# Top-k attention with a leaky-ReLU MLP: the first MLP chunks started earlier, half a layer summed ahead, two units scored later

## Chip, cores and metric

One core of a Trainium2 chip runs the whole program. The metric is device time in microseconds (us), as the median of repeated runs. Five engines take part, each with a queue that it works off in order: PE (TensorE, matrix products), DVE (VectorE), ACT (ScalarE), POOL (GpSimd) and SP, which only issues transfers here.

## What is computed

Attention over 8 batches, 8 heads, 576 tokens and head size 64, where each query keeps only the keys with its 32 highest scores; then a two-layer MLP over the 4608 tokens that this gives.

```python
scores = (1.0 / np.sqrt(D)) * np.matmul(q, k.transpose(0, 1, 3, 2))
kth = np.partition(scores, -32, axis=-1)[..., -32:-31]
scores = np.where(scores >= kth, scores, -1000000000.0)
scores = scores - np.max(scores, axis=-1, keepdims=True)
attn = np.exp(scores)
attn = attn / (np.sum(attn, axis=-1, keepdims=True) + 1e-09)
x = np.matmul(attn, v)              # (B, H, S, D) -> (B*S, H*D) = (4608, 512)
h = x @ w_in                        # w_in (512, 2048)
out = np.maximum(0.01 * h, h) @ w_out   # w_out (2048, 512)
```

All products are made in float32, which PE does in two passes; a matmul of the program is two rows of the profile.

## The kernel before

**Units and steps.** Heads go in pairs, four pairs a batch (`HP`). A unit is 128 query rows of both heads of one pair: 16 whole units a batch, and 2 made of the 64 rows left over from two pairs each, 144 units in all. Even batches have their whole units first, ordered by block of 128 queries and then by pair, so units 0 to 3 are the first 128 tokens of batch 0, 4 to 7 the next 128, 8 to 11 and 12 to 15 the last two blocks; 16 and 17 are its left-over units, 18 and 19 those of batch 1. The program is written out by a Python loop over steps `s` (L538), in an order fixed by hand. Every engine's queue gets its instructions in the order in which that loop emits them.

**What a step emits.** In step s DVE finds the top 32 of unit s (`top_k`, L243): it folds both halves of the scores to maxima and minima (L250), then four rounds of MAX8 (L255) and three of MATCH_REPLACE8 (L258); `slot()` emits one round, so a step has four slots. POOL masks unit s-1 (L268, L269, one pass for each head); ACT makes its exponents and their sums (`exponents`, L272; `sums`, tile `ze`, L277). Unit s-2 is divided by its sums: DVE's reciprocal (L281, tile `rz`) and ACT's normalising (L284), together `weights_of`. Then its weights are transposed, in one of two ways. `transpose` (L286) has ACT split them in two 16-bit halves (L293), SP store both to memory (L294) and a transfer bring them back transposed (L298, tile `wT`). `transpose_in_haste` (L300) has PE transpose nine blocks (L308), and ACT copy them out (`keep_transposed`, L314); units in `HASTY` go this way. Later, at the place that `values_at` (L449) gives, PE multiplies the transposed weights by the values (L335) for two units, and ACT copies the result to the MLP's input `x` (L349). A place is (step, MIDDLE) or (step, END). At the end of even steps PE makes the scores of the next two units (`scores`, L203: two tiles `wide`, and one `narrow` that both units share, L220), and ACT copies them out (L227). `first_scores` (L229) makes one unit's scores in two `wide` tiles without `narrow` (L236, L241); before, it serves units 0 and 1 only.

**Where the reciprocal stands.** `weights_of` comes at one of three spots of a step: ahead of the first slot for units in `HURRIED` below step 20 (`at_first`); after the first slot from step 20 on and in steps next to a hurried unit; after the second slot otherwise (`late`). DVE's queue is in order, so a reciprocal that has to wait for its sum holds up the top-k behind it.

**The MLP.** Tokens go in chunks: two of 128, then seventeen of 256 (`CHUNKS`). Chunk 0 needs units 0 to 3, chunk 1 units 4 to 7, chunk 2 (tokens 256 to 511) units 8 to 15. `mlp` is a generator that emits a few matmuls at a time: first layer (L359 and transposes L375 for the two small chunks, L391 for the others, tile `ph`), leaky ReLU by ACT (Prelu, L364 and L397, to `gT`), second layer (L403, tile `pz`), copy and store (L412, L413). A step has seven places at which `mlp_steps(budget)` lets it emit matmuls until the budget, counted in columns, is used up. Until chunk 2 is ready the budget is `EARLY_SHARE` a place; after that what is left is spread evenly over the steps until the next chunk is ready. A chunk becomes ready when its last values are copied (`attended`).

**On-chip accumulators.** The pool `ps_sc` has two buffers `wide` and one `narrow`, of two banks each; `ps_ml` has two of one bank for the MLP (tag `ml`). A tile that takes a buffer waits until the buffer's last reader is done.

The lines that set the places before:

```python
    LAG = 3
    HURRY = 20
    HURRIED = (15, 23, 31)
    HASTY = (14, 15, 23, 31)
    UNHURRIED = 14
    def values_at(n):
        if n < UNHURRIED:
            return (n | 1) + LAG + 1, MIDDLE
        return (n | 1) + LAG - ((n | 1) in HURRIED), END
```

Of the kernel before, what the change touches and what calls it, by code (L numbers as in the profile page):

```python
# [20 lines left out]
def kernel(  # L21
# [13 lines left out]
    nc = tc.nc  # L35
# [158 lines left out]
    units = []  # L194
    for b in range(B):
        first = b % 2 == 1
        whole = [Unit(b, [b * HP + hp], q0 + LEFT * first)
                 for q0 in range(0, S - LEFT, P) for hp in range(HP)]
        left = [Unit(b, [b * HP + hp, b * HP + hp + 1], 0 if first else S - LEFT)
                for hp in range(0, HP, 2)]  # L200
        units += left + whole if first else whole + left
# [27 lines left out]
    def first_scores(u):  # L229

        ps = [ps_sc.tile([P, 2, 512], F32, name="wide", bufs=2) for i in range(2)]
        for half in range(2):
            for i, pi, side, r0 in u.parts:
                qt, kt = qk_of[pi]
                d = slice(side * D, (side + 1) * D)
                nc.tensor.matmul(ps[i][:, half, 0:HS], qt[d, u.q0:u.q0 + P],  # L236
                                 kt[d, half * HS:(half + 1) * HS], start=True, stop=True)
        u.both = work.tile([P, 2, S], F32, name="s_sb", bufs=5)
        u.s = [u.both[:, i, :] for i in range(2)]
        for i in range(2):  # L240
            nc.scalar.copy(u.s[i].rearrange("p (h n) -> p h n", h=2), ps[i][:, :, 0:HS])  # L241
# [130 lines left out]
    def turned(j, g_of):  # L372
# [3 lines left out]
        nc.scalar.copy(gT[:, 4 * j:4 * (j + 1), 0:P], pt)  # L376
        yield 2 * P

    def mlp(ch):

        n = CHUNKS[ch]
        t0 = sum(CHUNKS[:ch])
        x = x_of[ch]
        if ch < EARLY:
            yield from hidden_of_few(ch, x)
        for f0 in range(0, NFC if ch >= EARLY else 0, 2):
            ph = ps_ml.tile([P, 2, CHMAX], F32, name="ph", tag="ml")
            for i in range(2):
                f = f0 + i
                for c in range(HP):  # L390
                    nc.tensor.matmul(  # L391
                        ph[:, i, 0:n], w_in[c][:, f * P:(f + 1) * P], x[c][:, 0:n],
                        start=(c == 0), stop=(c == HP - 1),
                    )
                    if c == 1 or i == 0 and c == HP - 1:
# [29 lines left out]
    def mlp_steps(budget):  # L425
        owed[0] += budget
        while owed[0] > 0:
            if running[0] is None:
                if not ready:
                    owed[0] = 0.0  # L430
                    return
                running[0] = mlp(ready.pop(0))
# [8 lines left out]

    LAG = 3
    HURRY = 20
    HURRIED = (15, 23, 31)
    HASTY = (14, 15, 23, 31)
    UNHURRIED = 14
    MIDDLE, END = 0, 1

    def values_at(n):  # L449

        if n < UNHURRIED:
            return (n | 1) + LAG + 1, MIDDLE
        return (n | 1) + LAG - ((n | 1) in HURRIED), END

    steps = units

# [11 lines left out]
    def attended(*place):  # L468
        for at, ch in ready_at:
            if at == place:  # L470
                ready.append(ch)
                backlog[0] += mlp_cost(ch)

    def slot_budget(s):

# [3 lines left out]
            return EARLY_SHARE  # L479
        return backlog[0] / ((until + 1 - s) * SLOTS)  # L480

    EARLY_SHARE = 500
    SLOTS = 7

    with tc.manual_schedule():
# [51 lines left out]

        for s in range(len(steps) + LAG + 1):  # L538
            cur, old, older, new = unit(s), unit(s - 1), unit(s - 2), ()
            if s % 2 == 0:  # L540
                new = [u for u in steps[s + 2:s + 4] if u]
            picks = top_k(cur) if cur else iter(())
            budget = slot_budget(s)

            def slot():
                next(picks, None)

            at_first = s < HURRY and s - 2 in HURRIED
            if at_first:
                weights_of(older)  # L550
            slot()
            if old:
                mask(old, 0)
                mask(old, 1)
            late = s < HURRY and not {s - 1, s - 2} & set(HURRIED)
            if older and not late and not at_first:
                weights_of(older)
            mlp_steps(budget)
            weighed = values(s, MIDDLE)
            at_once = s - 2 in HURRIED or any(at == (s, MIDDLE) for at, _ in ready_at)  # L560
# [24 lines left out]
            if new and s < HURRY:  # L585
                scores(new)
            keep(values(s, END), s, END)
            if new and s >= HURRY:
                scores(new)
            budget = slot_budget(s + 1)  # L590
            mlp_steps(budget)
            load_more(s)
# [59 lines left out]
```

## Time and profile before

| what | value |
|---|---|
| median of 6 runs | 1470.53 us (1469.16 to 1472.89) |
| the profiled execution | 1470.42 us, span 1468.5 us |
| PE busy | 1393.5 us (95%) |
| DVE busy | 1321.7 us (90%) |
| ACT, POOL busy | 1097.8 and 1096.1 us (75% each) |
| second layer, L403 | 504.7 us, 1152 passes |
| first layer of the large chunks, L391 | 482.6 us, 2176 passes |
| idle DVE ahead of the reciprocals, L281 | 45.3 us |

The span is what the profiler saw of the program's instructions; the execution's time holds some 2 us more around it. In the chain of work that ended last PE has 79% and DVE 14%. A row of the timeline gives start and length in us, engine, line, operation, output and inputs, shapes, the number of instructions merged, and in brackets idle time before and what ended it. A row of waits gives the engine that waited, for whom, the total, the number of times and the longest.

### The profile page before, as it was taken

The page shows a single profiled execution, that of the slowest core. Times are in us where ns is not written, and L with a number is a line of the kernel's source. Part 1 is how long each engine was busy: PE and PEld are TensorE (multiplying, and loading weights), DVE is VectorE, ACT ScalarE, POOL GpSimd, SP SyncE. Part 2 cuts the span into 40 slices and gives each one's busy share as a digit, 9 for nine tenths or more (in the row PEclk, how much of TensorE's full clock was granted, in tenths as well). Part 3 has the DMA queues.
Part 4 walks back from the last instruction along what each step waited for, and adds up shares of the span by engine and source line. Part 5 has one row for each costly group of instructions (what it writes and reads, how often), then busy time and mean ns, then how long its engine had stood idle before and what let it go on. Part 6 is the DMA issues. An engine that isn't in the chain of part 4 may idle for free.

```text
span 1468.5 us, 24096 instructions
## 1 busy us (share of the span) xinstructions
PE 1393.5 (95%) x8068; PEld 927.9 (63%) x8068; DVE 1321.7 (90%) x3400; ACT 1097.8 (75%) x1979; POOL 1096.1 (75%) x743
## 2 busy tenths in 40 slices
PE   7717999999999999999999999999999999999999
PEld 2304548575767676767676767666666666666674
DVE  7999999999999999999999999999999999999600
ACT  8657888777887777777777777777777777777710
POOL 3288888888788888788888887878787878787700
PEclk9957999999999999999999999999999999999999
DMA  9724443655376455664566555666457545554510
GB/s 347 284 74 129 144 120 100 187 145 144 96 193 190 137 137 155 171 185 137 146 165 187 149 137 138 179 178 152 124 163 207 137 137 138 162 139 135 146 47 14
DMA packets 388796, 222.30 MB, mean 151 GB/s; under 512 B 333888, under 2 KB 333889, under 8 KB 386625
## 3 DMA queue, kind: packets, MB, share of 16 engines
q1 hardware_dynamic: 388672, 220.77, 53.4%
q8 instruction: 63, 1.03, 0.3%
q14 instruction: 61, 0.49, 0.1%
HBM read 46.14 MB, written 92.01 MB: 94 GB/s over the span
## 4 chain that ended last, share of the span: by engine, by line
PE 79%; DVE 14%; DMA 3%; ACT 2%; issue 1%; SPq 0%; POOL 0%; DVEq 0%; ACTq 0%
PE pz L403 31%; PE ph L391 30%; PE wide L335 10%; DVE tops L255 6%; PE wide L220 6%; DVE pairs L258 5%; PE narrow L220 3%; DMA raw<-in_weights_dram 2%; DVE pairs L250 2%; DMA wT<-apart 1%; DMA apart<-split 0%; ACT split L293 0%; DVE scale L152 0%; DVE w_out L155 0%; ACT wT L127 0%
## 5 line engine op out<-in xcount | busy, mean ns | idle before, releaser
L268 POOL TENSOR_SCALAR pen<-s_sb,tops 128x576 f32<-128x576 f32 x288 | 637.5, 2213 | 208.6 <-DVE tops L255 139.3
L255 DVE MAX8 tops<-pairs 128x8 f32<-128x288 f32 (+1 forms) x1152 | 635.8, 591 | 0.0
L403 PE MATMUL pz<-w_out,gT 128*128 128x512 f32 x1152 | 504.7, 594 | 2.4 <-ACT scale L364 2.4
L391 PE MATMUL ph<-x,w_in 128*128 128x256 f32 x2176 | 482.6, 381 | 0.0
L258 DVE MATCH_REPLACE8 pairs<-tops,pairs 128x288 f32<-128x288 f32 (+1 forms) x864 | 460.1, 538 | 0.0
L391 PEld LDWEIGHTS ph<-x,w_in 128*128 128x128 f32 x2176 | 409.5, 190 | 76.4 <-issue 22.2
L269 POOL TENSOR_TENSOR s_sb<-s_sb,pen 128x576 f32<-128x576 f32 x288 | 406.5, 1411 | 24.1
L403 PEld LDWEIGHTS pz<-w_out,gT 128*128 128x128 f32 x1152 | 216.4, 190 | 267.2 <-issue 262.8
L293 ACT COPY split<-s_sb 128x1152 uint16<-128x1152 uint16 x280 | 309.4, 1146 | 0.0
L284 ACT ACTIVATE s_sb<-s_sb,rz 128x576 f32<-128x576 f32 x288 | 207.6, 773 | 45.2 <-DVE rz L281 45.1
L272 ACT ACTIVATE s_sb<-s_sb,nbias 128x576 f32<-128x576 f32 x288 | 222.2, 772 | 13.8 <-POOL s_sb L269 13.8
L250 DVE TENSOR_TENSOR pairs<-s_sb 128x576 f32<-128x576 f32 x288 | 213.4, 779 | 9.9
L335 PEld LDWEIGHTS wide<-wT,vt 128*64 128x64 f32 x3200 | 161.7, 139 | 67.5 <-issue 34.8
L335 PE MATMUL wide<-wT,vt 128*64 128x128 f32 (+1 forms) x3200 | 179.4, 268 | 25.5 <-ACT s_sb L227 22.2
L227 ACT COPY s_sb<-wide 128x704 f32<-128x704 f32 x142 | 107.1, 754 | 21.4 <-PE wide L220 21.4
L397 ACT ACTIVATE gT<-ph 128x512 f32<-128x512 f32 x136 | 80.6, 592 | 54.2 <-PE ph L391 53.4
L349 ACT COPY x<-wide 128x128 f32<-128x128 f32 (+1 forms) x160 | 32.2, 260 | 112.8 <-PE wide L335 112.8
L220 PE MATMUL wide<-kt,qt 64*128 64x352 f32 (+1 forms) x392 | 75.1, 493 | 26.0 <-ACT s_sb L227 23.5
L412 ACT COPY o_sb<-pz 128x512 f32<-128x512 f32 x36 | 21.0, 584 | 97.6 <-PE pz L403 97.6
L227 ACT COPY s_sb<-narrow 128x448 f32<-128x448 f32 x142 | 68.7, 536 | 0.7
L281 DVE RECIPROCAL rz<-ze 128x2 f32<-128x2 f32 x144 | 22.2, 154 | 45.4 <-ACT ze L277 45.3
L258 DVE MATCH_VALUE_LOAD pairs<-tops,pairs 128x8 f32 x864 | 62.5, 72 | 0.0
(63 smaller groups left out, 621.7 us busy)
## 6 DMA issues: line engine op xcount, KB each, us to landing
apart<-split SPq DMA_DIRECT2D x280, 288.0 KB, 2.1
raw<-in_weights_dram SPq DMA_DIRECT2D x16, 1024.0 KB, 6.9
vt<-in_vk_dram SPq DMA_DIRECT2D x32, 320.0 KB, 3.4
out_dram<-o_sb SPq DMA_DIRECT2D x36, 256.0 KB, 2.6
qt<-in_qT_dram SPq DMA_DIRECT2D x20, 288.0 KB, 3.1
kt<-in_kT_dram SPq DMA_DIRECT2D x20, 288.0 KB, 3.7
raw<-in_qT_dram SPq DMA_DIRECT2D x12, 288.0 KB, 3.2
raw<-in_kT_dram SPq DMA_DIRECT2D x12, 288.0 KB, 3.7
```

Of the source, the lines that this page charges most:

```text
L220: nc.tensor.matmul(to[r0:r0 + u.rows, i, :], qt[d, u.q0:u.q0 + u.rows], kt[d, k0:k1], start=True, stop=True)
L250: nc.vector.tensor_tensor(pairs[:, :, n, :], u.both[:, :, 0:HS], u.both[:, :, HS:S], op)
L255: nc.vector.max(out=u.tops[:, i, r, :], in_=rest[i])
L258: nc.vector.match_replace(out=rest[i], in_to_replace=u.tops[:, i, r, :], in_values=rest[i], imm_value=LOWEST)
L268: nc.gpsimd.tensor_scalar(pen, u.s[i], u.tops[:, i, ROUNDS - 1, 7:8], MASKED, ALU.is_lt, ALU.mult)
L269: nc.gpsimd.tensor_tensor(u.s[i], u.s[i], pen, ALU.add)
L272: nc.scalar.activation(u.s[i], u.s[i], AF.Exp, bias=u.nbias[:, i:i + 1], scale=SCALE, accum_out=u.z[:, i:i + 1])
L284: nc.scalar.activation(u.s[i], u.s[i], AF.Copy, bias=0.0, scale=u.rz[:, i:i + 1])
L293: nc.scalar.copy(split, pairs[:, :, h])
L335: nc.tensor.matmul(po[side * D:(side + 1) * D, o, :], vt[:, c, side, :], u.wT[:, c + side * NKC if c + 1 < NKC else c, r:r + n], start=(c ...
L391: nc.tensor.matmul(ph[:, i, 0:n], w_in[c][:, f * P:(f + 1) * P], x[c][:, 0:n], start=(c == 0), stop=(c == HP - 1),)
L403: nc.tensor.matmul(pz[0:m, 0:DMODEL], gT[:, f, r0:r0 + m], w_out[f // 4][:, f % 4, :], start=(f == 0), stop=(f == NFC - 1),)
```

## The change

- Chunks 0 and 1: units 2, 3 and 6, 7 join `HURRIED`, and their values are placed at (5, END) and (9, END) instead of (7, MIDDLE) and (11, MIDDLE). Units 0 to 3 and 7 join `HASTY`. `EARLY_SHARE` goes from 500 to 560.
- Units 8 to 15 are reordered so that a pair's two blocks follow each other: 8 and 9 are pair 0, 10 and 11 pair 1, and so on. So x of pairs 0 and 1 is complete over chunk 2 after unit 11, of pair 2 after 13, of pair 3 after 15.
- A new generator `begin_hidden` adds up the first half of chunk 2's first layer (8 of 16 blocks of w_in's columns) over pairs 0 and 1 from (15, MIDDLE), and over pair 2 from (17, MIDDLE). Four blocks lie in a `narrow` tile, four in both `ml` tiles, which they hold until `mlp` adds pair 3 and applies the leaky ReLU.
- As `narrow` is taken, units 18 and 19 are not scored at the end of step 16 by `scores`, but at the end of step 17, behind the values of units 14 and 15, by `first_scores`, which now also takes units of 64 rows.

```diff
+        tiles = [(0,), (P,), (2 * P, 3 * P)] if b == 0 else [(q0,) for q0 in range(0, S - LEFT, P)]
         whole = [Unit(b, [b * HP + hp], q0 + LEFT * first)
-                 for q0 in range(0, S - LEFT, P) for hp in range(HP)]
+                 for q0s in tiles for hp in range(HP) for q0 in q0s]
...
-                nc.tensor.matmul(ps[i][:, half, 0:HS], qt[d, u.q0:u.q0 + P],
+                nc.tensor.matmul(ps[i][r0:r0 + u.rows, half, 0:HS], qt[d, u.q0:u.q0 + u.rows],
                                  kt[d, half * HS:(half + 1) * HS], start=True, stop=True)
...
+    begun = {}
+
+    def begin_hidden(ch, pairs):
+        n = CHUNKS[ch]
+        x = x_of[ch]
+        if ch not in begun:
+            first = ps_sc.tile([P, 2, 512], F32, name="narrow").rearrange("p h (f n) -> p h f n", n=CHMAX)
+            begun[ch] = [first[:, 0], first[:, 1]]
+            begun[ch] += [ps_ml.tile([P, 2, CHMAX], F32, name="ph", tag="ml") for k in range(2)]
+        done = 0
+        for f in range(NFC // 2):
+            for c in pairs:
+                nc.tensor.matmul(begun[ch][f // 2][:, f % 2, 0:n], w_in[c][:, f * P:(f + 1) * P], x[c][:, 0:n],
+                                 start=(c == 0 and f % 2 == 0), stop=False)
+                done += 1
+                if done % 2 == 0:
+                    yield 2 * n
...
-            ph = ps_ml.tile([P, 2, CHMAX], F32, name="ph", tag="ml")
+            first = 0
+            if ch in begun and f0 < NFC // 2:
+                ph, first = begun[ch][f0 // 2], HP - 1
+            else:
+                ph = ps_ml.tile([P, 2, CHMAX], F32, name="ph", tag="ml")
             for i in range(2):
                 f = f0 + i
-                for c in range(HP):
+                for c in range(first, HP):
...
-    HURRIED = (15, 23, 31)
-    HASTY = (14, 15, 23, 31)
+    HURRIED = (3, 7, 15, 23, 31)
+    HASTY = (0, 1, 2, 3, 7, 14, 15, 23, 31)
     UNHURRIED = 14
+    LATE_SCORES = 17
...
-        if n < UNHURRIED:
-            return (n | 1) + LAG + 1, MIDDLE
-        return (n | 1) + LAG - ((n | 1) in HURRIED), END
+        if (n | 1) in HURRIED:
+            return (n | 1) + LAG - 1, END
+        return ((n | 1) + LAG + 1, MIDDLE) if n < UNHURRIED else ((n | 1) + LAG, END)
...
+        for last, pairs in ((11, (0, 1)), (13, (2,))):
+            if values_at(last) == place:
+                ready.append(begin_hidden(EARLY, pairs))
...
-    EARLY_SHARE = 500
+    EARLY_SHARE = 560
...
-            if s % 2 == 0:
-                new = [u for u in steps[s + 2:s + 4] if u]
+            if s % 2 == 0 and s != LATE_SCORES - 1:
+                new = steps[s + 2:s + 4]
+            elif s == LATE_SCORES:
+                new = steps[s + 1:s + 3]
...
-            at_once = s - 2 in HURRIED or any(at == (s, MIDDLE) for at, _ in ready_at)
+            at_once = s - 2 in HURRIED or s == values_at(11)[0] or any(at == (s, MIDDLE) for at, _ in ready_at)
...
-            if new and s < HURRY:
+            if new and s < HURRY and s != LATE_SCORES:
                 scores(new)
             keep(values(s, END), s, END)
             if new and s >= HURRY:
                 scores(new)
+            elif s == LATE_SCORES:
+                for u in new:
+                    first_scores(u)
```

More of the change, by code (lines that the diff above doesn't have):

```diff
@@ L386, in mlp @@
         for f0 in range(0, NFC if ch >= EARLY else 0, 2):
-            ph = ps_ml.tile([P, 2, CHMAX], F32, name="ph", tag="ml")
+            first = 0
[3 more added lines that the diff above has]
+                ph = ps_ml.tile([P, 2, CHMAX], F32, name="ph", tag="ml")
             for i in range(2):
                 f = f0 + i
-                for c in range(HP):
+                for c in range(first, HP):
                     nc.tensor.matmul(
                         ph[:, i, 0:n], w_in[c][:, f * P:(f + 1) * P], x[c][:, 0:n],
-                        start=(c == 0), stop=(c == HP - 1),
+                        start=(c == 0), stop=(c == HP - 1 and (i == 1 or not first)),
                     )
-                    if c == 1 or i == 0 and c == HP - 1:
+                    if not first and (c == 1 or i == 0 and c == HP - 1):
                         yield 2 * max(n, 225)
@@ L431, in mlp_steps @@
                     return
-                running[0] = mlp(ready.pop(0))
+                running[0] = ready.pop(0)
             cost = next(running[0], None)
@@ L470, in attended @@
             if at == place:
-                ready.append(ch)
+                ready.append(mlp(ch))
                 backlog[0] += mlp_cost(ch)
+        for last, pairs in ((11, (0, 1)), (13, (2,))):
+            if values_at(last) == place:
+                ready.append(begin_hidden(EARLY, pairs))
     def slot_budget(s):
```

## The prediction

> **What bounds the kernel now.** I number steps by the unit whose top-k runs in them; (17, END) is the end of step 17. First the windows, cut where chunks become ready (columns: busy us of PE, PEld, DVE, ACT, POOL, then granted clock).
>
> ```profile
> span 1468.5 us, 24096 instructions
> 64.90:117.80 52.90, 14.98 (x100) 11.05 (x100) 52.45 (x137) 29.33 (x52) 38.11 (x27) 0.61 0.25 68
> 117.80:224.30 106.50, 92.36 (x544) 51.19 (x546) 105.66 (x277) 86.19 (x166) 89.89 (x61) 0.94 0.46 128
> 224.30:295.20 70.90, 70.89 (x492) 49.79 (x487) 70.34 (x185) 56.06 (x109) 59.82 (x41) 1.00 0.54 148
> 295.20:369.00 73.80, 73.79 (x420) 50.35 (x419) 70.72 (x184) 55.57 (x105) 59.82 (x41) 1.00 0.52 144
> 369.00:453.00 84.00, 82.39 (x483) 55.84 (x484) 80.88 (x210) 66.90 (x126) 68.94 (x46) 1.00 0.55 156
> 453.00:1410.00 957.00, 956.42 (x5706) 654.00 (x5703) 890.94 (x2323) 746.41 (x1368) 760.82 (x509) 1.00 0.57 154
> ```
>
> From 453 on PE idles 0.6 us in 957: it is the bound, to the end. Before 118 DVE alone is full. So the question is when that full stretch begins. The chain of waits across 453 says (start, us, what):
>
> ```profile
> 439.01 2.10 ACT split L293 x2
> ...
> 441.13 4.21 DMA apart<-split
> ...
> 445.40 4.63 DMA wT<-apart
> ...
> 450.07 1.31 PE wide L335 x20
> ...
> 455.44 12.09 PE ph L391 x56
> ```
>
> At 450.07 PE waits for unit 39, the last of chunk 5, due at (42, END), and that unit hangs on DVE's step 41. Then DVE's own waits, in the window 224 to 455, and its step starts (first instruction of a top-k):
>
> ```profile
> DVE rz L281 <- ACT ze L277: 5.1, 5, 2.5
> ```
>
> ```profile
> 64.84 1.42 DVE L250 TENSOR_TENSOR pairs<-s_sb 128x576 f32<-128x576 f32 x2
> ...
> 224.26 1.45 DVE L250 TENSOR_TENSOR pairs<-s_sb 128x576 f32<-128x576 f32 x2
> ...
> 433.62 1.51 DVE L250 TENSOR_TENSOR pairs<-s_sb 128x576 f32<-128x576 f32 x2
> ```
>
> Undisturbed, DVE takes (224.26 - 64.84)/18 = 8.857 us a step; in the window 64 to 224 it waits for nothing. Step 41 would then start at 64.84 + 41 x 8.857 = 427.98 and starts at 433.62: **5.64 us lost, all of it after 224**, in reciprocals that wait for ACT's sums, ACT waiting in its queue for PE. The values at 450.07 come 16.45 after step 41's start, through ACT and two DMAs. That gives the **ceiling**: however much PE is relieved early, the full stretch can begin 5.64 sooner at most, and every DVE stall that the change adds before step 41 comes off that.
>
> PE's own rows:
>
> ```profile
> 110.81 4.53 PE L335 MATMUL wide<-wT,vt 128*64 128x128 f32 x40 [13.91 <-ACT s_sb L227]
> ...
> 149.34 2.40 PE L335 MATMUL wide<-wT,vt 128*64 128x128 f32 x40
> ...
> 210.55 1.43 PE L308 MATMUL wide<-ident,s_sb 128*128 128x128 f32 x9
> ...
> 223.77 2.40 PE L335 MATMUL wide<-wT,vt 128*64 128x128 f32 x40 [1.06 <-ACT wT L314]
> 226.10 7.17 PE L391 MATMUL ph<-x,w_in 128*128 128x256 f32 x32
> ```
>
> and one each of ACT, the copies of a whole unit's scores and a sum's end:
>
> ```profile
> 64.53 1.18 ACT L241 COPY s_sb<-wide 128x576 f32<-128x576 f32 x2 [5.86 <-PE wide L236]
> ...
> 139.61 0.20 ACT L277 ACTIVATE ze<-z 128x2 f32<-128x2 f32 x1
> ```
>
> **Part 1, the head start of chunk 2.** 24 matmuls (8 blocks of w_in by 3 pairs), two passes each, at 7.17/32 = 0.222 us (with overlap): 10.7 us leave steps 18 to 25. There PE takes 75.6 us (values at 223.77 to those at 299.36) against DVE's 8 x 8.857 = 70.9. Without 10.7, with the late scores (2.1 for two units: 217.07 to 219.17) added: 67.0, so DVE sets the pace there. Steps 26 to 33 keep 75.3 (299.36 to 374.65): PE falls 4.4 behind, where before it was 4.7 behind at step 26 with no stall yet. The nine steps of chunk 4 give that back. So of the 5.64 nearly all is open; stalls that stay: 0 to 1.1 (the first one of before, at 308), I take 0.3.
>
> **Part 2, units 18 and 19 late.** Their scores' last copy ended at 220.2, 4 before step 18; now they follow the values of 14 and 15. Times after step 17's start: POOL's mask of unit 16 is there at 3.15 (138.72 against 135.57 in step 8), the exponents take 0.95, then ACT copies unit 15's transposes (1.04): 5.2. PE meanwhile runs unit 15's nine transposes to 2.5 and the eight third-pair matmuls, 16 x 0.222 = 3.55, to 6.05. Values 2.35: 8.4. ACT copies them (0.43) to 8.85; the second tile of unit 18 is the one that they leave, so its scores (1.05) end at 9.9, and both copies (1.18) at 11.1. Step 18 should start at 8.86: **late by 2.3 plus some hops, 2.6 taken**. No gain is possible; at worst the eight matmuls slip behind ACT's copy as well, 4.5. Queued behind: DVE's whole stream, POOL's masks; unit 19's scores wait for unit 18's copies, but are due a step later.
>
> **Part 3, chunks 0 and 1 sooner.** Units 0 to 3 and 7 lose two split copies (2.10 of ACT), two stores and a DMA transpose each, and gain nine PE transposes (1.27 to 1.43) and one pair of copies (1.18). SP's queue only loses entries; loads behind them go out sooner at most. At (5, END) and (9, END) ACT's copies of the values wait for PE, and behind them in ACT's queue stand the next step's normalising and exponents, which the reciprocals need. PE has the room: 14.98 busy of 52.9. Values of 2 and 3 move from step 7 to (5, END), some 13 us earlier, of 6 and 7 from step 11 to (9, END). 560 columns a place: 1024 stand for four passes of 512, 4 x 0.438 = 1.75 us, so 7 places ask 6.7 us a step instead of 6.0. With 1.17 of values and 1.07 of scores PE has 8.94 a step where DVE takes 8.86 (8.24 before): full, 0.7 over in nine steps, 1.3 more for unit 7's transposes.
> This is paid where DVE meets ACT. Step 9 now begins with unit 7's reciprocal, step 5 with unit 3's, and in steps 4 and 8 the reciprocal moves a slot forward, from 4.5 to 2.95 after the start. In step 8 the sum came at 139.81; the new place is at 135.57 + 2.95 = 138.52, up to 1.3 too soon. From there ACT has normalise 1.35, one gT copy 0.47, exponents 0.76, splits 2.10, exponents and sum 1.1: 144.3 at the earliest, just when step 9's reciprocal wants it (144.27), so 0.2 to 0.4 late. Step 5 has copies of 1.04 in place of splits and fits. In steps 10 to 14 sums came 1.2 to 4.5 after the step's start, with 4.5 allowed; a PE some 2 us behind pushes some over. Bounds 0.2 and 4, **1.5 taken**, nearer to the low end as units 10 to 15 leave ACT time to catch up.
>
> The clock: the same 40 passes took 4.53 after 13.9 idle and 2.40 in a full stretch. With transposes and scores just ahead I take 3.2 for the first values in step 5; it lies within the 1.5. [...]
>
> **Part 4, the rest.** The units' order and the score tile's rows change no count. Two accumulators in the score tile and both others are held from step 15 to 18: chunk 1 is done by then (62 places of 560 from (5, END): step 14), and no scores fall between. If it were not, see the third rival.
>
> **Sum**: 5.64 - 0.3 - 2.6 - 1.5 = 1.2 won. The profiled execution took 1470.42 around its span of 1468.5, the median is 1470.53: **1469.3 us**, no change that can be told (0.2%, 2.9 us, is about what a measurement of this kernel can tell from none). Own range, with all lower and all upper bounds: 5.64 less 2.5 to 9.6, so 1467.3 to 1474.4.
>
> **Rivals.**
> Faster: the reciprocals cost nothing and steps 26 to 41 have no stall. Then 5.64 - 2.3 is won: 1467.1. For it: ACT is busy 86 of 106 us in 118 to 224. Against: step 9's tight chain. To be clearly faster, part 3 may cost 0.3 at most.
> Slower: the full PE of steps 6 to 14. Each Prelu in ACT's queue waits for PE, each sum behind it comes late, DVE waits, one step after another. It decides from 2.8 of stalls in steps 5 to 17 on (with 2.6 and 0.3, all of 5.64), and at 1 us a step in steps 8 to 14 it costs 7: 1470.4 + 7 + 2.6 + 0.3 - 5.64 = 1474.7. For it: 8.94 against 8.86, and 4.5 allowed where 4.5 was used. Against: in steps 26 to 34 PE ran 4.7 behind before DVE lost its first microsecond.
> The head start that isn't: chunk 1 ends only in step 16, the begun sums wait for its buffers, and half of their first 7.1 us stands before the values of 14 and 15: step 18 late by 2.6 + 3.5 rather than 2.6, 1472.7. For it: PE full from step 6 on; against: two steps between 14 and 16.
>
> **Chances.** Forecast 0.47, faster 0.20, slower 0.27, no head start 0.06. Faster by over 0.2%: 0.20; within: 0.47 and a little of the others, 0.48; slower: 0.32. Eight times in ten: 1466.8 to 1474.8.
>
> **What would show it.** Step 18's first DVE row 2.3 to 3 later than 8.86 after step 17's, waiting for ACT's score copies; reciprocals that wait in steps 8, 9 and some of 10 to 14, none before; no DVE wait in 18 to 26; PE idle in 18 to 25, some 4 us in all; the first matmul of chunk 5 at about 454. Wrong, if the end moves without that matmul moving, or if step 41 starts before 430.3 (64.84 + 41 x 8.857 + 2.3).

## The result and the profile after

The changed kernel takes 1474.02 us, the kernel before 1471.35 in the same comparison (medians of 19 and 41 runs): ratio 1.002, interval 1.0014 to 1.0026. That is a small, sure loss of some 2.9 us, where the forecast was a small win at 1469.3. The profiled execution took 1476.84 (span 1475.1). Lines have moved: the top-k now begins on L252 (L250 before), the reciprocal is on L283, the values are on L337, the second layer on L429, the sums ahead on L395; L243 is the score copy of `first_scores`.

The windows of the changed kernel, cut at the same events as before (step 6, step 18, step 26, step 34, the scores behind chunk 5's last values), the last one to a length close to that of before (columns: busy us of PE, PEld, DVE, ACT, POOL, then granted clock).

```profile
span 1475.1 us, 24166 instructions
...
119.80:231.70 111.90, 104.51 (x600) 61.23 (x596) 105.75 (x277) 84.51 (x162) 93.36 (x63) 0.98 0.37 101
231.70:302.95 71.25, 65.81 (x429) 41.85 (x429) 70.29 (x184) 57.08 (x109) 56.21 (x39) 0.98 0.53 147
302.95:374.20 71.25, 71.24 (x414) 49.21 (x413) 70.47 (x184) 54.42 (x100) 59.85 (x41) 1.00 0.55 149
374.20:456.70 82.50, 80.68 (x469) 54.37 (x468) 79.37 (x208) 65.70 (x122) 67.47 (x46) 1.00 0.55 151
456.70:1413.00 956.30, 955.28 (x5677) 652.85 (x5676) 892.56 (x2325) 746.74 (x1368) 762.26 (x509) 1.00 0.57 154
```

In the long last window PE is full as it was (idle 1.0 of 956.3 us), so the question is again when it begins. In steps 18 to 25 PE is now idle for 5.4 us, as wanted, and the granted clock is 0.98 in the first two windows shown. DVE's waits from step 0 to there, in the changed kernel (who waits, for whom: total, times, longest), and three step starts:

```profile
DVE rz L283 <- ACT ze L279: 4.4, 6, 2.5
DVE pairs L252 <- ACT s_sb L243: 3.9, 1, 3.9
DVE pairs L252 <- ACT ze L279: 0.5, 1, 0.5
```

```profile
66.85 1.42 DVE L252 TENSOR_TENSOR pairs<-s_sb 128x576 f32<-128x576 f32 x2
...
231.68 1.48 DVE L252 TENSOR_TENSOR pairs<-s_sb 128x576 f32<-128x576 f32 x2 [3.87 <-ACT s_sb L243]
...
438.81 1.51 DVE L252 TENSOR_TENSOR pairs<-s_sb 128x576 f32<-128x576 f32 x2
```

I call the **loss at step s** its start, less step 0's start, less 8.857 s. At step 41 it is 438.81 - 66.85 - 363.14 = 8.82, where the kernel before had 5.64: 3.2 us later, about the measured loss. It comes in three pieces: 1.6 by step 17, 3.8 at step 18, 3.4 between 18 and 41. The sum of the prediction had 1.5, 2.6 and 0.3.

The chain of waits of the changed kernel shows the late start of the full stretch (start, us, what); chunk 5's first long group of matmuls, at 455.44 before, is at 460.85, of which 2.0 is a later step 0 (66.85 for 64.84). That start varies from execution to execution: in the kernel before, profiled a second time, it was 66.29. So places are compared after step 0. The spans of the two profiled executions differ by 6.6: 2.0 is the later step 0, 3.2 the loss at step 41, and 1.4 lies behind step 41 (1.9 between the second profiles of both kernels). Idle PE is 0.4 and 1.0 of that; the rest was not taken apart.

```profile
450.82 4.61 DMA wT<-apart
...
455.48 1.31 PE wide L337 x20
...
460.85 9.28 PE ph L417 x43
```

### The profile page after: what moved, and what is told of

The parts are those of the page before. It is cut to its first block, busy times and chain, and to the rows that moved or that the text cites. A ratio compares the mean times of both kernels' runs of the same rounds, so it can differ in the third digit from the quotient of the medians.

```text
span 1475.1 us, 24166 instructions
## 1 busy us (share of the span) xinstructions
PE 1405.8 (95%) x8113; PEld 934.2 (63%) x8113; DVE 1321.8 (90%) x3400; ACT 1094.4 (74%) x1979; POOL 1096.1 (74%) x743
## 4 chain that ended last, share of the span: by engine, by line
PE 82%; DVE 9%; DMA 5%; ACT 3%; issue 1%; POOL 0%; DVEq 0%; SPq 0%; POOLq 0%; ACTq 0%
PE pz L429 31%; PE ph L417 29%; PE wide L337 10%; PE wide L222 6%; DVE tops L257 4%; DVE pairs L260 3%; PE narrow L222 3%; DMA wT<-apart 2%; DMA raw<-in_weights_dram 2%; DVE pairs L252 1%; PE ph L361 1%; ACT split L295 1%; DMA apart<-split 1%; ACT wT L127 0%; DVE w_out L155 0%
## 5 line engine op out<-in xcount | busy, mean ns | idle before, releaser
L429 PE MATMUL pz<-w_out,gT 128*128 128x512 f32 x1152 | 504.9, 595 | 0.9 <-ACT scale L366 0.9
L417 PE MATMUL ph<-x,w_in 128*128 128x256 f32 x2120 | 470.5, 381 | 0.9 <-ACT gT L423 0.9
L417 PEld LDWEIGHTS ph<-x,w_in 128*128 128x128 f32 x2120 | 398.9, 190 | 75.6 <-issue 22.1
L429 PEld LDWEIGHTS pz<-w_out,gT 128*128 128x128 f32 x1152 | 216.3, 190 | 266.7 <-issue 263.0
L295 ACT COPY split<-s_sb 128x1152 uint16<-128x1152 uint16 x270 | 299.0, 1146 | 0.0
L252 DVE TENSOR_TENSOR pairs<-s_sb 128x576 f32<-128x576 f32 x288 | 213.2, 779 | 14.0 <-ACT s_sb L243 3.9
L337 PEld LDWEIGHTS wide<-wT,vt 128*64 128x64 f32 x3200 | 159.6, 138 | 53.6 <-issue 36.4
L337 PE MATMUL wide<-wT,vt 128*64 128x128 f32 (+1 forms) x3200 | 178.9, 267 | 10.4 <-DMA wT<-apart 6.3
L283 DVE RECIPROCAL rz<-ze 128x2 f32<-128x2 f32 x144 | 22.2, 154 | 45.9 <-ACT ze L279 45.8
```

The source lines that it names most:

```text
L252: nc.vector.tensor_tensor(pairs[:, :, n, :], u.both[:, :, 0:HS], u.both[:, :, HS:S], op)
L295: nc.scalar.copy(split, pairs[:, :, h])
L337: nc.tensor.matmul(po[side * D:(side + 1) * D, o, :], vt[:, c, side, :], u.wT[:, c + side * NKC if c + 1 < NKC else c, r:r + n], start=(c ...
L417: nc.tensor.matmul(ph[:, i, 0:n], w_in[c][:, f * P:(f + 1) * P], x[c][:, 0:n], start=(c == 0), stop=(c == HP - 1 and (i == 1 or not first)),)
L429: nc.tensor.matmul(pz[0:m, 0:DMODEL], gT[:, f, r0:r0 + m], w_out[f // 4][:, f % 4, :], start=(f == 0), stop=(f == NFC - 1),)
```

## The experiments

All are variants of the two kernels. The table has the loss at steps 17, 18 and 41, the start of the values at (25, END) after step 0's start, and the time: the median beside that of the kernel before in the same comparison. "560" and "500" are `EARLY_SHARE`.

| kernel | 17 | 18 | 41 | (25, END) | us (before) | ratio, interval |
|---|---|---|---|---|---|---|
| before | 0.0 | 0.0 | 5.6 | 234.5 | | |
| before, second profile | -0.1 | 0.0 | 5.6 | 234.5 | 1470.9 (one run) | |
| changed | 1.6 | 5.4 | 8.8 | 237.7 | 1474.02 (1471.35) | 1.002, 1.0014 to 1.0026 |
| changed, again | 1.6 | 5.6 | 9.0 | 237.8 | 1474.13 (1471.29) | 1.0019, 1.001 to 1.0028 |
| e1 chunks 0, 1 sooner only, 560 | 1.3 | 1.3 | 5.9 | 234.7 | 1473.35 (1471.94) | 1.0011, 1.0003 to 1.002 |
| e9 the same, 500 | 1.8 | 1.8 | 7.4 | 236.3 | 1472.02 (1471.49) | 1.0006, 0.9996 to 1.0016 |
| e2 late scores only | -0.1 | 2.7 | 8.2 | 237.0 | 1474.39 (1471.94) | 1.0014, 1.0005 to 1.0023 |
| e3 unit 18 ahead of values | 1.6 | 1.6 | 7.0 | 235.9 | 1474.15 (1471.94) | 1.0014, 1.0005 to 1.0022 |
| e4 chunk 2 done by step 24 | 1.7 | 4.0 | 8.0 | 236.0 | 1477.74 (1471.94) | 1.0039, 1.0027 to 1.0052 |
| e10 both | 1.6 | 2.6 | 10.4 | 236.9 | 1475.37 (1471.49) | 1.0023, 1.0012 to 1.0034 |
| e5 changed with 500 | 1.8 | 6.1 | 9.5 | 238.3 | 1474.46 (1471.34) | 1.0021, 1.0012 to 1.0031 |
| e6 half the head start, 560 | 1.6 | 1.7 | 4.7 | 231.9 | 1470.78 (1471.34) | 1.0, 0.9991 to 1.0009 |
| e7 half, 500 | 0.4 | 0.4 | 3.5 | 230.7 | 1470.96 (1471.34) | 0.9997, 0.9988 to 1.0006 |
| e8 a quarter, 500 | 1.6 | 1.6 | 5.8 | 234.2 | 1471.98 (1471.49) | 1.0003, 0.9995 to 1.0012 |
| e12 changed, tighter spread | 1.6 | 3.9 | 6.3 | 235.2 | 1472.97 (1471.29) | 1.0015, 1.0006 to 1.0024 |
| e13 e3 and tighter spread | 1.6 | 1.6 | 3.6 | 232.5 | 1470.68 (1471.29) | 0.9991, 0.9982 to 1.0 |
| e11 half, 500, tighter spread | 0.4 | 0.4 | 2.3 | 230.6 | 1469.00 (1471.49) | 0.998, 0.9971 to 0.9988 |
| e15 before, tighter spread | 0.2 | 0.1 | 7.1 | 235.9 | 1472.02 (1471.29) | 1.0002, 0.9994 to 1.0011 |

**One part alone (e1, e2).** e1 is the changed kernel without the head start and the late scores; e2 is the kernel before with only the late scores.

```diff
e1:
-    LATE_SCORES = 17
+    LATE_SCORES = -1
...
-        for last, pairs in ((11, (0, 1)), (13, (2,))):
-            if values_at(last) == place:
-                ready.append(begin_hidden(EARLY, pairs))
...
-            at_once = s - 2 in HURRIED or s == values_at(11)[0] or any(at == (s, MIDDLE) for at, _ in ready_at)
+            at_once = s - 2 in HURRIED or any(at == (s, MIDDLE) for at, _ in ready_at)
e2, in the kernel before:
...
+    LATE_SCORES = 17
...
-            if s % 2 == 0:
-                new = [u for u in steps[s + 2:s + 4] if u]
+            if s % 2 == 0 and s != LATE_SCORES - 1:
+                new = steps[s + 2:s + 4]
+            elif s == LATE_SCORES:
+                new = steps[s + 1:s + 3]
...
-            if new and s < HURRY:
+            if new and s < HURRY and s != LATE_SCORES:
...
+            elif s == LATE_SCORES:
+                for u in new:
+                    first_scores(u)
```

The expectations of e1 and e2:

> Leaves out the head start of chunk 2 and the late scores; keeps chunks 0 and 1 sooner and 560 columns. Theory (what costs is DVE's 3.8 us wait for unit 18's scores, and what was won on PE idles away in steps 18 to 25): DVE loses 1 to 2 us in steps 8 to 13 as in the changed kernel, nothing at step 18, and PE's values at (25, END) come 3 to 4 us after step 26's start as before; time 0 to 1 us over before, 1471.4 to 1472.4. Rival (the full PE of steps 6 to 14 is what costs): as slow as the changed kernel, 1474.

> The kernel before with units 18 and 19 scored behind the values of 14 and 15, and nothing else. Theory: step 18 starts 4 to 5 us late, which is more than PE's lead there takes up, so the values at (25, END) follow DVE: 2 to 3 us slower than before, 1473.5 to 1474.5. Rival (DVE loses 5.6 us to PE until step 36 anyway, so a late step 18 only takes the place of those waits): at most the 1.3 us that PE itself waits for score copies, 1472.5 or less.

e1 is a little slower than before (by 0.4 to 2.9 us) and loses 1.3 by step 17, as expected; at step 41 only 0.2 of it is left in its trace, as a later DVE finds PE less behind at step 26 (3.0 for 4.2 before). e2 loses 2.7 at step 18, which is the prediction's 2.6 and not the 4 to 5 expected here; at step 41 it has lost 2.5 more than before, and its time is as expected. So each side effect alone has about its forecast price in time (1.4 and 2.5); what is missing is what the head start should have won.

**Taking the two suspects away one by one (e3, e4, e10).** e3 scores unit 18 ahead of the values of units 14 and 15. e4 spreads chunk 2's work so that it ends in step 24 rather than 25. e10 does both.

```diff
e3:
             if not older or s - 2 in HASTY:
                 mlp_steps(budget)
+            if s == LATE_SCORES:
+                first_scores(new[0])
...
             elif s == LATE_SCORES:
-                for u in new:
-                    first_scores(u)
+                first_scores(new[1])
e4:
-        return backlog[0] / ((until + 1 - s) * SLOTS)
+        ahead = until - s if s < until <= 25 else until + 1 - s
+        return backlog[0] / (ahead * SLOTS)
```

The expectations of e3, e4 and e10:

> The changed kernel with unit 18 alone scored one spot earlier, ahead of the values of units 14 and 15 (its copies ahead of unit 16's second exponents); unit 19 stays behind them. Theory: step 18's wait of 3.9 goes, everything from step 18 to (25, END) comes 3.8 sooner: 1470.2 (1469.5 to 1471). Rival (the time is set by PE, which has lost nothing there): no change, 1474, as the values of 14 and 15 and so chunk 2 come 1 to 2 us later.

> The changed kernel with chunk 2's matmuls spread over steps 18 to 24 instead of 18 to 25. Theory: PE's 5.9 us of idle time in steps 18 to 25 shrink to about 2, the values at (25, END) come 3 to 4 us sooner against step 26's start, the 2.5 us wait of step 35 goes or shrinks, DVE still loses 5.4 by step 18: 1471.0 (1470.3 to 1472). Rival (DVE's late start of step 18 alone decides): 1474.

> The changed kernel with unit 18 scored ahead of the values of 14 and 15, and with chunk 2's work spread over steps 18 to 24. Theory (both waits of the change lie in the order of things, not in its amount of work): loss at step 18 1.4 to 1.7, values at the end of step 25 1 to 2 after step 26's start, loss at step 41 4.5 to 5.2, time 1470.5 to 1472 if before stands at 1471.3. Rival (finishing chunk 2 early only moves its last copy in front of the exponents in ACT's queue, and PE falls empty behind it): values at the end of step 25 at 236 after step 0 again, loss at step 41 6.5 or more, time 1473.5 to 1476.

All three theories failed. e3's time is its rival's. In e3 step 18 no longer waits, but DVE then loses 5.4 between 18 and 41 instead of 3.4: of the 3.8, 2.0 come back as stalls, since the values at (25, END) are only 1.8 sooner. Its PE rows show part of why: the transposed weights of one unit come late, PE stands still, and what follows runs at about half rate (the same 20 passes take 1.31 elsewhere, the four score passes 0.86; the granted clock is 0.68 from 284 to 294).

```profile
288.10 2.40 PE L337 MATMUL wide<-wT,vt 128*64 128x128 f32 x20 [2.66 <-DMA wT<-apart]
290.43 1.55 PE L222 MATMUL wide<-raw 64*128 64x352 f32 x4
```

In e10 the rival held. ACT's rows, then PE's:

```profile
300.68 0.59 ACT L438 COPY o_sb<-pz 128x512 f32<-128x512 f32 x1 [4.26 <-PE pz L429]
...
301.94 1.17 ACT L316 COPY wT<-wide 128x1024 f32<-128x1024 f32 x2
```

```profile
297.30 3.35 PE L429 MATMUL pz<-w_out,gT 128*128 128x512 f32 x4
302.99 3.30 PE L337 MATMUL wide<-wT,vt 128*64 128x128 f32 x34 [2.34 <-ACT wT L316]
```

Chunk 2's last copy (`o_sb`) now stands in ACT's queue ahead of unit 23's transposed weights (`keep_transposed`). ACT waits 4.26 in it for PE, and then PE waits 2.34 for ACT, idle ahead of the values at (25, END). Ending a whole step early is too early. That e4's time is 6 us above before, when its trace has 2.4 more lost by step 41, is explained in part only: 1.7 to 2.7 more lie behind step 41.

**Less of the head start (e5 to e9).** e6 and e7 sum only the four blocks in the `ml` accumulators ahead (5.3 us of PE), so `narrow` stays free and units 18 and 19 are scored as before. e8 sums two blocks in one accumulator. e5 is the whole change with 500, e9 is e1 with 500. A control profiles the kernel before a second time. e8 is e7 with one `ml` tile in place of two and `NFC // 8` in place of `NFC // 4`.

```diff
e6, e7 (e7 also EARLY_SHARE = 500):
-            first = ps_sc.tile([P, 2, 512], F32, name="narrow").rearrange("p h (f n) -> p h f n", n=CHMAX)
-            begun[ch] = [first[:, 0], first[:, 1]]
-            begun[ch] += [ps_ml.tile([P, 2, CHMAX], F32, name="ph", tag="ml") for k in range(2)]
+            begun[ch] = [ps_ml.tile([P, 2, CHMAX], F32, name="ph", tag="ml") for k in range(2)]
...
-        for f in range(NFC // 2):
+        for f in range(NFC // 4):
...
-            if ch in begun and f0 < NFC // 2:
+            if ch in begun and f0 < NFC // 4:
...
-    LATE_SCORES = 17
+    LATE_SCORES = -1
```

The expectations of the control, then of e5 to e9 in order:

> The kernel before, unchanged, for one more profiled execution. In the first one step 0 began at 64.84; in the changed kernel and three of its variants it began between 65.8 and 66.9, though nothing ahead of step 0 differs. Theory (the start only varies from execution to execution): step 0 may begin anywhere between 64.8 and 67, and from there to the end of the span it is again 1403.7, within 1; the values at the end of step 25 come 234.5 after step 0's start, within 0.5. Rival (the change itself costs some 2 us ahead of step 0): step 0 at 64.8 within 0.4.

> The changed kernel with 500 columns a place until chunk 2 is ready, as before, in place of 560. Theory (most of the 1.6 us that DVE loses in steps 11, 12 and 16 is PE being too full to give ACT its tiles in time, and the halved clock around step 17 comes from PE running empty once chunk 1 is done early): DVE loses at most 0.8 by step 17, chunk 1 ends in step 15 or 16, and step 18 waits 2.3 rather than 3.8; loss at step 18 about 3, time 1.5 to 2 below the changed kernel's: 1472.3 if before stands at 1471.9. Rival (the reciprocals pulled forward for units 3 and 7 are what costs; the columns are nothing): loss at step 17 again 1.6, at step 18 5.4, time 1474.5; and if the begun sums now wait for chunk 1's buffers, step 18 is later still, 1476.

> The changed kernel with half its head start: only the four blocks that lie in the two MLP accumulators are summed ahead (12 matmuls, 5.3 us), so the score tile stays free and units 18 and 19 are scored at the end of step 16 as before. Theory (the loss of the change is the wait of step 18; what can be won is only what brings the values at the end of step 25 forward): no wait at step 18, DVE lag there 1.3 to 1.6 as with the chunks alone; the values at the end of step 25 some 1.5 to 2 after step 26's start, 233.5 to 234 after step 0 (234.5 before, 237.7 in the changed kernel), and the time 0.5 to 1 below before, 1471.1 if before stands at 1471.9. Rival (head start costs by itself, by PE falling to half rate in the idle it makes): values at 235.5 or later, time 1473 to 1474.

> As the one before, and 500 columns a place in place of 560. Theory: the loss of steps 11 to 16 falls below 0.8 as well, chunk 1 ends in step 15 or 16 and the begun sums follow it at once; values at the end of step 25 some 232.5 to 233.5 after step 0, time 1470.3 if before stands at 1471.9, the fastest of all. Rival (500 brings nothing, or the begun sums come too late and push the values of 14 and 15): as the one before or up to 2 slower.

> As the half head start at 500 columns, but only two of the sixteen blocks are summed ahead, in one MLP accumulator (6 matmuls, 2.7 us). With the half, DVE lost 3.1 between step 18 and step 41, with the whole (10.7 us) 3.4, with none 5.6. Theory (the head start saturates: as soon as the values at the end of step 25 come within 2 of step 26's start, only the 2.6 at step 35 and a few tenths are left, and no further relief of steps 18 to 25 takes them away): 2.9 to 3.3 lost between 18 and 41 also here, values at the end of step 25 some 1 to 2.2 after step 26's start, time within 0.8 of the half's, 1470.6 to 1471.8 if before stands at 1471.3. Rival (each microsecond moved counts alike, as my prediction had it): halfway between none and half, 4.2 to 4.5 lost, time 1 above the half's.

> Only the earlier values of chunks 0 and 1, with 500 columns; no head start, no late scores. Theory (the 560 columns are what costs in steps 11, 12 and 16): DVE loses 0.3 to 0.6 by step 17, then 5.3 between 18 and 41 as before, 5.7 to 5.9 in all, time that of before within 0.7: 1471.3. Rival (the reciprocals pulled forward cost, whatever the columns, as the 1.76 in one of the runs with 500 says): 1.4 to 1.8 by step 17, 1473.

The control's first theory held: step 0 starts anywhere, and the rest is the same within 1.0. Half the head start brings the values to 231.9 and 230.7, earlier than the whole one (237.7) by some 6 to 7; further than I expected, and both kernels are level with before (e7 was to be 1 us faster). A quarter is worth less than half: 4.1 lost between 18 and 41, against 3.1, so my theory of an early saturation failed and its rival, that each microsecond counts, held about up to the half (4.1, where it had 4.2 to 4.5). Beyond it the whole head start still leaves 3.4.

e5 fell out as its rival had it, in numbers: 1.8, 6.1 and 1474.5. Step 18 waits 4.3 with a granted clock of 1.00 there (205 to 231), because chunk 1 ends late and begun sums, pushed behind it, now stand ahead of the values of units 12 and 13 in step 17. The 500 columns divide the executions: loss at step 17 is 0.4 in e7 and e11 and 1.6 to 1.8 in e5, e8 and e9, with the same order up to step 15. That is the clock (eight passes in 5.23 to 5.40 us against 3.70, last section), not the reciprocals alone, as e9's rival had it. With 560 it was 1.3 to 1.7 in all nine executions.

**A tighter spread (e11 to e15).** Chunk 2's work is spread as if it were due 0.3 of a step earlier, rather than e4's whole step. e11 is e7 with it, e12 the changed kernel, e13 is e3, e15 the kernel before; e14 is the changed kernel profiled again.

```diff
-        return backlog[0] / ((until + 1 - s) * SLOTS)
+        ahead = until + 0.7 - s if until == 25 else until + 1 - s
+        return backlog[0] / (ahead * SLOTS)
```

The expectations of e11 to e15, in order:

> The half head start at 500 columns, with chunk 2's work spread as if it were due a third of a step earlier. With the even spread its last four passes of the second layer (1.8 us) came behind the values at the end of step 25, while PE had been idle 4.3 us in steps 18 to 25. Theory (the idle can take them): values at the end of step 25 within 0.5 of where they were (230.6 after step 0), the values at the end of step 33 some 1.2 to 1.8 sooner (306 to 306.6 after step 0; 307.65 there), loss at step 41 2.3 to 3.2, time 1469.5 to 1470.5 if before stands at 1471.3, the fastest of all. Rival (the passes only come ahead of the values, which are then 1.8 later): nothing is won, 1470.9.

> The changed kernel with chunk 2's work spread as if due a third of a step earlier, nothing else. Theory (the even spread is half of the loss: it leaves PE idle in steps 18 to 25 and its last passes ahead of the values at the end of step 25): those values 1 to 2 sooner, 235.7 to 236.7 after step 0 (237.7 in the changed kernel), loss at step 41 7 to 8, time 1 to 1.5 below the changed kernel's: 1473 if before stands at 1471.4. Rival (the wait of step 18 is all of it; a tighter spread only moves idle): 237.4 or later, 1474.3 or more.

> The changed kernel with unit 18 scored ahead of the values of 14 and 15 and the tighter spread. Theory (wait of step 18 and spread together are the whole loss): no wait at step 18, loss there 1.4 to 1.8; values at the end of step 25 233.3 to 234.8 after step 0; loss at step 41 4.5 to 6; time 1470.8 to 1472, at least as fast as before. Rival (a whole head start is too much: chunk 2 has too little left to keep PE busy until step 25, and PE runs empty and then at half rate): 235.5 or later, 1473.5 to 1475.

> The changed kernel again, unchanged. Theory (its parts are the same from execution to execution but for the clock): loss at step 17 1.3 to 1.8, wait of step 18 2.2 to 3.9, values at the end of step 25 236.3 to 238 after step 0, loss at step 41 7.3 to 9; time 1.0014 to 1.0026 of before. Rival (the first profile was one unlucky execution): loss at step 41 at most 6.5.

> The kernel before with the tighter spread of chunk 2's work, nothing else. Theory (PE has no idle from 224 to 299 there, so nothing can be taken forward; the gain of the half head start with this spread comes from both together): values at the end of step 25 234.4 to 235.5 after step 0, loss at step 41 5.4 to 6.2, time within 0.8 of before. Rival (the spread by itself is the gain): values at the end of step 33 at least 1 sooner than 309.8 after step 0, time 1469.5 to 1470.3 if before stands at 1471.4.

e12 and e13 met their theories, in the trace even beyond them. The changed kernel loses 2.5 less at step 41 with the spread, but 1.5 of that is there at step 18 already, where the spread has not begun: the wait is 2.2 in this execution and 3.8 in the changed kernel's, by the clock (see part 2 below). Between 18 and 41 the spread takes off 1.0 (3.4 to 2.4), and the medians lie some 1.1 apart. Without the wait of step 18 another 2.7 go. Here the removed wait is not given back, as it was in e3: from e3 to e13, which start step 18 alike, the spread takes the loss between 18 and 41 from 5.4 to 2.0. DVE waits in e12, then in e13:

```profile
DVE rz L283 <- ACT ze L279: 2.8, 5, 1.1
DVE pairs L252 <- ACT s_sb L243: 2.3, 1, 2.3
DVE pairs L252 <- ACT ze L279: 0.5, 1, 0.5
```

```profile
DVE rz L283 <- ACT ze L279: 3.0, 6, 1.2
DVE pairs L252 <- ACT ze L279: 0.5, 1, 0.5
```

e14 repeats the loss and its three pieces (1.6, 3.9, 3.4). In e15 the spread alone wins nothing; it moves PE's lag into steps 18 to 25, where DVE then stalls (7.1 at step 41, more than I expected). **e11 beats both kernels**: 0.998, interval 0.9971 to 0.9988, some 2.9 us below before (1.8 to 4.3). Its values at the end of step 33 start 306.5 after step 0 (309.8 before, 313.0 in the changed kernel, 307.7 in e7). PE rows of e11 up to (25, END), then DVE's waits from step 0 to step 42:

```profile
284.44 2.60 PE L337 MATMUL wide<-wT,vt 128*64 128x128 f32 x40
...
292.02 1.43 PE L310 MATMUL wide<-ident,s_sb 128*128 128x128 f32 x9 [0.93 <-ACT s_sb L286]
293.29 3.60 PE L427 MATMUL pz<-w_out,gT 128*128 128x512 f32 x8
296.82 2.40 PE L337 MATMUL wide<-wT,vt 128*64 128x128 f32 x40
```

```profile
DVE rz L283 <- ACT ze L279: 2.4, 2, 1.7
```

Eight passes, not twelve, stand between the transposes and the values, no weights come late, and the values start where step 26 does (296.92). The half head start with 560 columns and this spread was not run, so what the 500 adds to e11 is not known.

## Why the prediction went wrong, by its own steps

**The ceiling held, the exchange roughly.** The late start of step 41 largely sets the time: 3.2 later by the trace in the changed kernel was 2.9 in the measurement, 3.3 sooner in e11 was 2.9. But from step 41 to the end the two profiles of before take 1034.9 and 1033.9 us, those of the changed kernel 1036.3 and 1035.8, that of e11 1036.1, so the exchange is good to some 1 to 2 us. Where the trace gains less (e6 and e7: 0.9 and 2.1 at step 41), the measurement can't tell it from nothing: in their steady part short waits for transposed weights, 0.9 and 1.2 us from 460 on against 0.6 and 0 in the two profiles of before, take some of it.

**Part 3, the chunks sooner: right in size.** 1.5 forecast, 1.6 measured. The places were right in part: DVE waited in steps 11 and 12, which "some of 10 to 14" covers, and in 16, but hardly in 8 and not in 9. As the cause of these waits was not taken apart, the agreement in size may be luck.

**Part 2, the late scores: the mechanism right, the size of this execution not.** 2.6 forecast, 3.8 measured, again 3.9 in e14, but 2.2 in e12 and e4, with the same order up to step 18. The difference is PE's rate: the granted clock from 205 to 231 is 0.93 in the changed kernel and in e14, 1.00 in e12 and e4. First the changed kernel, then e12:

```profile
216.72 1.31 PE L337 MATMUL wide<-wT,vt 128*64 128x128 f32 x20 [0.99 <-ACT wT L316]
218.84 2.19 PE L337 MATMUL wide<-wT,vt 128*64 128x128 f32 x20 [0.81 <-DMA wT<-apart]
220.97 1.94 PE L310 MATMUL wide<-ident,s_sb 128*128 128x128 f32 x9
```

```profile
215.47 1.31 PE L337 MATMUL wide<-wT,vt 128*64 128x128 f32 x20 [0.99 <-ACT wT L316]
217.63 1.31 PE L337 MATMUL wide<-wT,vt 128*64 128x128 f32 x20 [0.85 <-DMA wT<-apart]
218.88 1.24 PE L310 MATMUL wide<-ident,s_sb 128*128 128x128 f32 x9
```

Two short idles, and the second twenty passes take 2.19 or 1.31, the nine transposes 1.94 or 1.24: 1.6 of step 18's wait. The prediction looked for the clock in step 5 only (its first 40 value passes took 2.40, at 113.30, for the 3.2 estimated), not where its own change would make PE stop.

**Part 1, "stalls that stay 0.3": the step that failed.** Measured 3.4: 0.4 by step 26, 0.4 from there to step 34, 2.6 from there to step 41. Its working took "67.0, so DVE sets the pace there" to mean that PE comes to step 26 level, falls "4.4 behind" in steps 26 to 33, and that this costs nothing, as before was "4.7 behind at step 26 with no stall yet". The fall of 4.4 held (4.0); the other two are wrong.

First, PE does not come level. PE rows ahead of (25, END), of the kernel before, then of the changed kernel:

```profile
294.12 5.32 PE L403 MATMUL pz<-w_out,gT 128*128 128x512 f32 x12
299.36 2.40 PE L335 MATMUL wide<-wT,vt 128*64 128x128 f32 x40
```

```profile
287.39 1.31 PE L337 MATMUL wide<-wT,vt 128*64 128x128 f32 x20
290.88 2.40 PE L337 MATMUL wide<-wT,vt 128*64 128x128 f32 x20 [2.18 <-DMA wT<-apart]
293.21 1.33 PE L222 MATMUL wide<-raw 64*128 64x352 f32 x4
...
299.32 5.32 PE L429 MATMUL pz<-w_out,gT 128*128 128x512 f32 x12
304.57 1.64 PE L337 MATMUL wide<-wT,vt 128*64 128x128 f32 x26
```

What is left of chunk 2 is spread evenly until the end of step 25, whatever is left. With 10.7 us less of it PE idles between the pieces (5.4 in steps 18 to 25, 2.18 of it ahead of 290.88, then half rate: a granted clock of 0.50 from 290.90 to 293.20), and the last 12 of the 64 passes of chunk 2's second layer still stand between unit 23's transposes, which wait for step 25's normalising, and the values. These start 1.6 after step 26 (302.96), where before it was 4.2: of the 4.2 to be made up, 2.6 are. The half rate is not the reason. In e5, where the granted clock is 1.00 from 270 to 310 and PE idles 6.7 in steps 18 to 25, they also start 1.6 after step 26 (302.22):

```profile
297.32 1.43 PE L310 MATMUL wide<-ident,s_sb 128*128 128x128 f32 x9 [1.24 <-ACT s_sb L286]
298.59 5.32 PE L429 MATMUL pz<-w_out,gT 128*128 128x512 f32 x12
303.83 2.40 PE L337 MATMUL wide<-wT,vt 128*64 128x128 f32 x40
```

With eight passes there, in e11, e12 and e13, PE is level with step 26.

Second, being some 5 behind is not free. At (33, END) PE is 5.6 behind step 34 (379.86 against 374.24), and ACT's rows there say what that costs:

```profile
379.97 0.58 ACT L438 COPY o_sb<-pz 128x512 f32<-128x512 f32 x1 [3.08 <-PE pz L429]
382.31 0.43 ACT L351 COPY x<-wide 128x128 f32<-128x128 f32 x2 [1.76 <-PE wide L337]
```

Both copies wait for PE, and the next step's normalising, exponents and sum stand behind them in ACT's queue; DVE's reciprocal in step 35 waits 2.50 for that sum, just as in the kernel before (first the changed kernel, then before):

```profile
388.62 0.17 DVE L283 RECIPROCAL rz<-ze 128x2 f32<-128x2 f32 x1 [2.50 <-ACT ze L279]
```

```profile
383.42 0.17 DVE L281 RECIPROCAL rz<-ze 128x2 f32<-128x2 f32 x1 [2.50 <-ACT ze L277]
```

The kernel before had such waits after step 26 too: 1.06 at 308.12 and 0.46 at 317.54. I read "4.7 behind with no stall yet" as a lag that is free. It was 4.2, the first stall came one step later, and the free part is smaller. Take PE's lag as the start of the values at (33, END) less that of step 34, and set it beside what DVE loses from step 34 to step 41:

| profiles | PE's lag | DVE loses |
|---|---|---|
| e12, e13 | 4.3 | 1.2 |
| e11 | 4.8 | 1.8 |
| e8, e15 | 5.2 | 2.2 |
| both of before, both of the changed kernel, e1, e2, e3, e5, e9 | 5.6 | 2.6 |
| e6, e7 | 6.0 | 2.9 |
| e4, e10 | 5.2 | 2.55 |

In all but the last row the loss is the lag less 3.0: so much is free there, and the rest counts one for one. At (25, END) 1.2 is free in the same way, in the nine profiles with the even spread and the whole head start or none: before, a lag of 4.2 costs 3.0, in the changed kernel 1.6 costs 0.4. That is why both kernels are 5.6 behind at step 34: DVE waits off what exceeds 1.2, and steps 26 to 33 add 4.4, as they hold more PE work (75.3 us) than DVE time (70.9). With 1.6 of lag left, the head start could shorten only the first of the two stalls, and a PE level with step 26 would still have lost 1.2 in step 35, as e12 and e13 do.

With the measured terms the sum 5.64 - 3.4 - 3.8 - 1.6 comes to 3.2 lost, where it had 1.2 won; 3.1 of the 4.4 between is part 1, 1.2 is part 2.

**The rivals.** "Slower: the full PE of steps 6 to 14" gave nearly the right time (1474.7) for a wrong reason: steps 5 to 17 cost 1.6, not 7. "The head start that isn't" did not cost anything with 560, though chunk 1 ended at the turn to step 16 and not in step 14; e5 is it, with 500.

What stays open: why the reciprocals of steps 11 and 12 wait with 560 columns in every execution was not taken apart. How often the slower clock falls into steps 17 and 25 is known from these profiles only.

## What to carry to other kernels

Work taken off an engine is worth only what reaches the next due point: look at what stands in front of that point after the change, and if a planner spreads the rest evenly up to it, retune the spread with the load (here 1.0 us of stalls with the late scores, 3.4 with unit 18 scored sooner; a spread a whole step tighter cost more time than it won). If half of a change needs none of its side effects, try the half: four blocks in accumulators that were free anyway beat eight that displaced two units' scores (e11 against e12, whose `EARLY_SHARE` differs too). A lag that shows no wait yet is not all slack; find the next in-order queue in which its copies stand ahead of somebody else's work, and read from several variants how much lag it takes there for free (here 1.2 and 3.0 us).

## What the runs showed of the hardware

PE's granted clock fell, in the changed kernel to 0.50 (290.90 to 293.20) and 0.55 (218.90 to 220.90), after idles of 2.4 us and less, and not every time. Five executions with 500 columns had the same order up to step 15; in each PE was idle for 2.4 us and then ran eight passes of the second layer. First e5, then e7, each with its window 140 to 150 (the clock follows POOL's busy time):

```profile
141.28 5.40 PE L429 MATMUL pz<-w_out,gT 128*128 128x512 f32 x8 [2.39 <-ACT scale L366]
```

```profile
140.00:150.00 10.00, 8.71 (x27) 4.13 (x28) 9.33 (x26) 8.01 (x16) 8.62 (x6) 0.83 0.63 163
```

```profile
140.85 3.70 PE L427 MATMUL pz<-w_out,gT 128*128 128x512 f32 x8 [2.39 <-ACT scale L366]
```

```profile
140.00:150.00 10.00, 9.15 (x54) 5.02 (x56) 9.33 (x25) 8.81 (x16) 8.62 (x6) 1.00 0.71 176
```

It was 5.40, 5.23 and 5.40 in e5, e8 and e9, 3.70 in e7 and e11. Behind the 1.7 us, DVE waits for ACT's sums in steps 11 and 12 of e5, e8 and e9 (0.4 to 0.6 each) and not in e7 and e11: loss at step 17 of 1.6 to 1.8 against 0.4. Beside these, a lower rate followed idles of 2.18 and, at step 17, of 0.99 and 0.81 close together in the changed kernel, and of 2.66 in e3; in e12 it did not follow 0.99 and 0.85. One and the same idle of 2.4 us was followed by slower passes in three executions and not in two, so its length alone does not say which comes; what does was not shown.
